# A pooled-attention and MLP kernel with its prologue rearranged: PSUM banks by hand, v in two parts, and small loads on other queues

## The chip, the cores and the metric

The kernel runs on one core of a Trainium2 chip. The metric is the device time of one execution in microseconds. The profile of one execution shows five engines: TensorE (PE, matmuls; PEld is its weight load), VectorE (DVE), ScalarE (ACT), GpSimd (POOL) and SyncE (SP), and sixteen DMA engines that they share. SP, ACT and POOL issue DMAs, each on a queue of its own: in the profile q1 is SyncE's, q10 ScalarE's and q0 GpSimd's.

## The reference

Eight batches of attention with eight heads; keys and values are averaged over groups of eight positions first. The result, one row of 512 numbers for each of 8 x 576 tokens, goes through an MLP with `h - tanh(h)` in the middle.

```python
batch, n_heads, seq, head_dim = (8, 8, 576, 64)      # pool = 8, so 72 pooled keys
k_p = k.reshape(B, H, Sp, pool, D).mean(axis=3)
v_p = v.reshape(B, H, Sp, pool, D).mean(axis=3)
scores = scale * np.matmul(q, k_p.transpose(0, 1, 3, 2))
attn = softmax(scores)                                # cut
attn_out = np.matmul(attn, v_p)
x = attn_out.transpose(0, 2, 1, 3).reshape(B * S, H * D)   # 4608 x 512
h = x @ w_in                                          # 512 x 2048
out = (h - np.tanh(h)) @ w_out                        # 2048 x 512
```

## The kernel before

Tokens are taken in nine groups of 512 for the MLP. For groups 1 to 8 the attention of the next batch is worked in between the MLP's matmuls. Group 0 has nothing before it, so the kernel opens with a prologue: load k, q and v of batch 0, pool and transpose them, compute scores, attention and x, and begin the MLP, while w_in (`w1b`), w_out (`w2b`) and batch 1 are on their way. `warm_pe` issues matmuls on zeros as filler for TensorE.

The loads of the prologue, in the order of the program (each engine runs its own in this order):

```python
# SyncE: keys of batch 0; ScalarE: queries of batch 0 but for the last 64 rows
load_main(k_pairs, k_raw[0], 0, 0, 1);  load_q0(0, 2)
load_main(k_pairs, k_raw[0], 0, 1, 2);  load_q0(2, 4)
load_main(k_pairs, k_raw[0], 0, 2, 4);  load_q0(4, 8)
load_dense(k_pairs, k_raw[0], 0, nc.scalar)
load_dense(v_pairs, v_raw[1], 0, nc.scalar)
...
nc.gpsimd.dma_start(out=v_bf[:, 0:NM, :], in_=v_pairs[0, 0:128, :, :])
...
for c in range(4):
    load_w1(c)                       # GpSimd: a quarter of w_in each, cast to bf16
load_w2(0)
nc.gpsimd.tensor_copy(out=v_bf[:, NM, :], in_=v_raw[1][:, NM, :])
load_w2(1)
nc.gpsimd.memset(k_raw[1][:, NM, :], 0.0)
nc.gpsimd.memset(v_raw[0][:, NM, :], 0.0)
nc.gpsimd.memset(KB[1][:, :], 0.0)

q_raws[1] = raw.tile(...)
after(load_k(1), w1_dmas[1])         # SyncE: keys of batch 1, once w1's second quarter is in
load_q(1, False)                     # SyncE
load_main(v_pairs, v_raw[1], 1, 0, NM)
```

The compute of the prologue:

```python
q_turn(...); k_turn(...); q_pe_transpose(...)         # cut
scores_wide(0, (0, 1))
nc.scalar.dma_start(out=t0[:QT, :, R, :], in_=q[0, :, QA:S, :].rearrange("h p d -> p h d"))
...                                                   # scores of the other keys, v pooled
load_left(v_pairs, v_raw[1], 1, nc.scalar)            # four small loads of batch 1
load_q_tail(1, q_raws[1], nc.scalar)

warm_pe(2, b0=3)
av_pair(0, 0, 2)                  # attention times v for two blocks of 128 tokens, one half
av_pair(1, 0, 5)                  # of the heads; VectorE then divides by the sum
av_pair(0, 1, 0)
warm_pe(1)
x0_turn((0, 1), 0, 7, nc.scalar.copy)   # transpose x by PE, copy it into xT
av_pair(1, 1, 2)
warm_pe(1)
x0_turn((2, 3), 0, 5, nc.scalar.copy)
warm_pe(2)
h_open(3, 4)                      # two of the four matmuls of an MLP tile, on 512 tokens
x0_turn((0, 1), 1, 7, nc.scalar.copy)
h_open(0, 0)
h_open(1, 1)
x0_turn((2,), 1, 5, nc.scalar.copy)
x0_turn((3,), 1, 6, nc.vector.tensor_copy)
h_open(2, 2)
h_open(4, 3)
nc.scalar.copy(out=q_bf[:QT, R, :, :], in_=t0[:QT, :, R, :])   # L740: cast of q's tail
for i in range(5):
    mlp_h_mms(0, i, 2, 4)         # the other two matmuls of the tile (L453)
    mlp_h_act(i, gts)             # ScalarE: tanh (L464); VectorE: gT = h - tanh(h) (L466)
for i in range(5, NHID):
    mlp_h(0, i, gts)              # all four matmuls; three PSUM banks in turn (ps_h)
    if i == 7:  q_pe_tail(0)      # reads q_bf's tail
    ...
pool_k(1, nc.gpsimd, mid=(2, 3))  # GpSimd: keys of batch 1, with load_w2(2), (3) in between
after(load_k(2), w2_dmas[2])
...
for u in range(16):               # second MLP product (L481), with batch 1's attention between
    ...
```

Of the kernel before, what the change touches and what calls it, by code (L numbers as in the profile page):

```python
# [8 lines left out]
FP32 = mybir.dt.float32  # L9
# [5 lines left out]
B, H, S, D = 8, 8, 576, 64  # L15
# [22 lines left out]
def kernel(  # L38
# [22 lines left out]
    def bank(i, shape):  # L61
        n = 1
        for d in shape[1:]:
            n *= d
        v = PS[:, i, 0:n]
        if len(shape) == 3:
            return v.rearrange("p (a b) -> p a b", a=shape[1])
        if len(shape) == 4:
            return v.rearrange("p (a b c) -> p a b c", a=shape[1], b=shape[2])
        return v  # L70
# [6 lines left out]
            self.n += 1  # L77
            return bank(self.ids[(self.n - 1) % len(self.ids)], shape)

    ps_h = Banks(0, 1, 2)  # L80
    ps_o = Banks(3, 4)
    ps_a = Banks(5, 6, 7)

    ctx.enter_context(tc.manual_schedule())

# [19 lines left out]
    VB = [const.tile([128, 3 * NM, D1], BF16, name=f"VB{i}") for i in range(2)]  # L105

    q_raws = {}
    rot = [0]

    def ps_any(shape, dtype, name):  # L110
        pool, tag = [(ps_a, "ps_a"), (ps_h, "hT_ps")][rot[0] % 2]
        rot[0] += 1
        return pool.tile(shape, dtype, name=name, tag=tag)

    evac_n = [0]

# [7 lines left out]
    def load_main(src, dst, b, t0, t1):  # L124
        return nc.sync.dma_start(out=dst[:, t0:t1, :], in_=src[b, 0:128, t0:t1, :])

    def load_left(src, dst, b, eng=nc.sync):
        return [
            eng.dma_start(out=dst[32 * t : 32 * t + LO, NM, :], in_=src[b, 128:PR, t, :])
            for t in range(NM)  # L130
        ]
# [17 lines left out]
    def load_q_tail(b, t, eng):  # L149
        eng.dma_start(  # L150
            out=t[:QT, :, R, :], in_=q[b, :, QA:S, :].rearrange("h p d -> p h d")
        )

    def load_q(b, tail=True):
        if b not in q_raws:
            q_raws[b] = raw.tile([128, H, R + 1, D], FP32, name="q_raw", tag="q_raw")
        t = q_raws[b]
        nc.sync.dma_start(
            out=t[:, :, 0:R, :], in_=q[b, :, 0:QA, :].rearrange("h (p j) d -> p h j d", j=R)
        )  # L160
        if tail:
            load_q_tail(b, t, nc.sync)

    qTs = {}
    kdups = {}
# [82 lines left out]
        v_main(VB[b % 2], r[:, :, 0:1, :], eng, 0, NM)  # L248
        v_left(VB[b % 2], r[:, NM, 0:1, :], eng)

    def v_main(vb, vs, eng, t0, t1):
        n = t1 - t0
        eng.tensor_tensor(
            out=vb[:, 2 * t0 : 2 * t1, 0:D].rearrange("p (t s) d -> p t s d", s=2),
            in0=vs[:, t0:t1, :, :].to_broadcast([128, n, 2, D]),
            in1=mask[:, 2 * t0 : 2 * t1, :]
            .rearrange("p (t s) o -> p t s o", s=2)
            .to_broadcast([128, n, 2, D]),
            op=ALU.mult,
        )  # L260

    def v_left(vb, vs, eng):
        eng.tensor_tensor(
            out=vb[:, 2 * NM :, 0:D],
            in0=vs.to_broadcast([128, NM, D]),
            in1=mask[:, 2 * NM :, :].to_broadcast([128, NM, D]),
            op=ALU.mult,
        )
# [179 lines left out]
    def mlp_h_mms(g, i, f0, f1, pool=None):  # L448
        tok0 = g * TG
        if f0 == 0:  # L450
            h_tiles[i] = ps_h.tile([128, TG]) if pool is None else pool
        for fb in range(f0, f1):
            nc.tensor.matmul(  # L453
                h_tiles[i][:, :],
                lhsT=w1b[:, fb, i * 128 : (i + 1) * 128],
                rhs=xT[:, fb, tok0 : tok0 + TG],
                start=(fb == 0),
                stop=(fb == NFB - 1),
            )

    def mlp_h_act(i, gts):
# [71 lines left out]
    def load_w2(c):  # L533
        w2_dmas.append(
            nc.gpsimd.dma_start(  # L535
                out=w2b[:, c * 4 : (c + 1) * 4, :], in_=w2_src[:, c * 4 : (c + 1) * 4, :]
            )
        )

    def after(lds, dep):  # L540
        for ld in lds:
            tc.add_manual_dep(
                ld.ins,
                dep.ins.name,
                mybir.DependencyInfo(mybir.DependencyClass.Sync, mybir.DependencyReason.DATA),
            )

    def warm_pe(n, cols=512, b0=4):
        for _ in range(n):
            nc.tensor.matmul(  # L550
                bank(b0, [128, cols]), lhsT=zeros[:, 0:128], rhs=zeros[:, 0:cols], start=True, stop=True
            )
# [52 lines left out]
    for c in range(4):  # L605
        load_w1(c)
    load_w2(0)
    nc.gpsimd.tensor_copy(out=v_bf[:, NM, :], in_=v_raw[1][:, NM, :])
    load_w2(1)
    nc.gpsimd.memset(k_raw[1][:, NM, :], 0.0)  # L610
    nc.gpsimd.memset(v_raw[0][:, NM, :], 0.0)
    nc.gpsimd.memset(KB[1][:, :], 0.0)

    q_raws[1] = raw.tile([128, H, R + 1, D], FP32, name="q_raw", tag="q_raw")
    after(load_k(1), w1_dmas[1])
    load_q(1, False)
    load_main(v_pairs, v_raw[1], 1, 0, NM)

    def k_turn(ta, tb):
# [5 lines left out]
    def k_turn_left():  # L625
        ps = ps_any([128, 128], FP32, "kT_ps")
        turn_tile(ps[:, :], kdups[0], NM)
        kb_left(KB[0], ps, nc.vector.tensor_copy)
# [3 lines left out]
    def q_turn(eng, h0, h1):  # L632
        eng(
            out=q_bf[:, 0:R, h0:h1, :].rearrange("p j h d -> p h j d"),
            in_=t0[:, h0:h1, 0:R, :],
        )

    def v_pe_pool(t0, t1, turn, b0=None):
        shape = [128, t1 - t0, 1, D]
        ps = ps_any(shape, FP32, "v_ps") if b0 is None else bank(b0, shape)  # L640
        for j in range(POOL):
            nc.tensor.matmul(
                ps[:, :, 0, :],
                lhsT=turn[:, :],
                rhs=v_bf[:, t0:t1, j * D : (j + 1) * D],
                start=(j == 0),
                stop=(j == POOL - 1),
            )
        return ps

    def ps_b1(shape, dtype, name):
        return ps_a.tile(shape, dtype, name=name, tag="ps_a")

    q_turn(nc.scalar.copy, 0, 2)
    q_turn(nc.scalar.copy, 2, 4)
    k_turn(0, 1)
    q_pe_transpose(0, (0,), "act")
    warm_pe(1)
    k_turn(1, 2)
    q_pe_transpose(0, (1,), "act")  # L660
    warm_pe(2)
    scores_wide(0, (0, 1))
    nc.scalar.dma_start(out=t0[:QT, :, R, :], in_=q[0, :, QA:S, :].rearrange("h p d -> p h d"))
    q_turn(nc.scalar.copy, 4, 6)
    q_turn(nc.scalar.copy, 6, 8)
    pool_k(0, nc.vector, 2, 4)
    warm_pe(6)
    k_turn(2, 4)
    pool_k(0, nc.vector, NM, NT)
    warm_pe(2)  # L670
    q_pe_transpose(0, (2, 3), "act")
    warm_pe(2)
    scores_wide(0, (2, 3))
    k_turn_left()
    warm_pe(2)
    v_ps = v_pe_pool(NM, NT, spread)
    scores_wide(0, (NM,))
    v_left(VB[0], v_ps[:, 0, :, :], nc.vector)
    vs = v_pe_pool(0, NM, ident, 4)
    v_main(VB[0], vs, nc.vector, 0, 2)  # L680
    v_main(VB[0], vs, nc.vector, 2, 4)
    load_left(v_pairs, v_raw[1], 1, nc.scalar)
    load_q_tail(1, q_raws[1], nc.scalar)
    gts = []

    def av_pair(p, half, b0):
        ps = PS[:, b0 : b0 + 2, 0 : 4 * D1].rearrange("p k (h d) -> p k h d", d=D1)
        for k in range(2):
            av_mms(0, 2 * p + k, half, ps[:, k, :, :])
        rden = work.tile([128, 2, 4, 1], FP32, name="rden2", tag="rden2")  # L690
        nc.vector.reciprocal(out=rden[:, :, :, :], in_=ps[:, :, :, D:D1])
        nc.vector.tensor_tensor(
            out=x0[:, 2 * p : 2 * p + 2, half, :, :],
            in0=ps[:, :, :, 0:D],
            in1=rden[:, :, :, :].to_broadcast([128, 2, 4, D]),
            op=ALU.mult,
        )
# [16 lines left out]
            in_=ps.rearrange("p f i c -> p f (i c)"),  # L714
        )

    def h_open(i, b0):
        mlp_h_mms(0, i, 0, 2, bank(b0, [128, TG]))

    warm_pe(2, b0=3)  # L720
    av_pair(0, 0, 2)
    av_pair(1, 0, 5)
    av_pair(0, 1, 0)
    warm_pe(1)
    x0_turn((0, 1), 0, 7, nc.scalar.copy)
    av_pair(1, 1, 2)
    warm_pe(1)
    x0_turn((2, 3), 0, 5, nc.scalar.copy)
    warm_pe(2)
    h_open(3, 4)  # L730
    x0_turn((0, 1), 1, 7, nc.scalar.copy)
    h_open(0, 0)
    h_open(1, 1)
    x0_turn((2,), 1, 5, nc.scalar.copy)
    x0_turn((3,), 1, 6, nc.vector.tensor_copy)
    h_open(2, 2)
    h_open(4, 3)
    ps_any = ps_b1
    ps_h.n = ps_o.n = 0
    nc.scalar.copy(out=q_bf[:QT, R, :, :], in_=t0[:QT, :, R, :])  # L740
# [113 lines left out]
```

The softmax here doesn't subtract the row's maximum and nothing guards it: scores larger than these inputs give would overflow.

## Time and profile before

| | |
|---|---|
| time, median of three runs | 300.99 us (300.81 to 301.04) |
| span of the profiled execution | 299.0 us |
| PE busy | 291.5 us (97%) |
| DVE, ACT, POOL busy | 158.4, 148.8, 115.7 us |
| HBM read, written | 36.70 MB, 9.44 MB |

A row of the timeline has the start in microseconds from the span's beginning, the length, the engine (with a q behind it: its sequencer, issuing a DMA), the line, the operation, what it writes and reads, the count, and in brackets how long the engine had been idle and what ended that. A row of the waits has who waited for whom, the total in microseconds, how often, and the longest. The landing of a DMA is counted from its issue.

### The profile page before, as it was taken

The page shows a single profiled execution, that of the slowest core. Times are in us where ns is not written, and L with a number is a line of the kernel's source. Part 1 is how long each engine was busy: PE and PEld are TensorE (multiplying, and loading weights), DVE is VectorE, ACT ScalarE, POOL GpSimd, SP SyncE. Part 2 cuts the span into 40 slices and gives each one's busy share as a digit, 9 for nine tenths or more (in the row PEclk, how much of TensorE's full clock was granted, in tenths as well). Part 3 has the DMA queues.
Part 4 walks back from the last instruction along what each step waited for, and adds up shares of the span by engine and source line. Part 5 has one row for each costly group of instructions (what it writes and reads, how often), then busy time and mean ns, then how long its engine had stood idle before and what let it go on. Part 6 is the DMA issues. An engine that isn't in the chain of part 4 may idle for free.

```text
span 299.0 us, 4704 instructions
## 1 busy us (share of the span) xinstructions
PE 291.5 (97%) x1672; PEld 142.8 (48%) x1672; DVE 158.4 (53%) x336; ACT 148.8 (50%) x279; POOL 115.7 (39%) x110
## 2 busy tenths in 40 slices
PE   7999999999999999999999999999999999999994
PEld 3454355544544454445544554455445544444443
DVE  5658665673547444753476247715680758008600
ACT  4647583666146623664266416651666066126511
POOL 8600906770396109913971099208930000000000
PEclk9999999999999999999999999999999999999999
DMA  7999999749955995699648974895431630111033
GB/s 259 221 211 280 310 235 328 233 89 331 233 109 109 290 283 129 109 297 250 105 89 236 313 166 88 265 294 137 89 66 35 90 96 0 37 70 36 2 70 70
DMA packets 66183, 49.79 MB, mean 167 GB/s; under 512 B 39920, under 2 KB 52976, under 8 KB 66160
## 3 DMA queue, kind: packets, MB, share of 16 engines
q1 hardware_dynamic: 58832, 42.94, 55.5%
q0 software_dynamic: 4752, 4.72, 9.5%
q10 hardware_dynamic: 2576, 1.84, 2.2%
q8 instruction: 13, 0.21, 0.3%
q14 instruction: 10, 0.08, 0.1%
HBM read 36.70 MB, written 9.44 MB: 154 GB/s over the span
## 4 chain that ended last, share of the span: by engine, by line
PE 85%; DMA 9%; POOL 4%; issue 0%; SPq 0%; ACT 0%; DVE 0%; POOLq 0%; DVEq 0%
PE PS L481 40%; PE PS L453 37%; DMA w1b<-in_moe_w_in_dram 4%; PE PS L368 4%; DMA k_raw<-in_k_dram 4%; PE PS L321 3%; POOL k_raw L221 1%; DMA out_dram<-o_sb 1%; POOL k_raw L226 1%; POOL kd L229 1%; POOL w2b L535 0%; PE PS L416 0%; POOL v_raw L599 0%; PE PS L194 0%; POOL w1b L528 0%
## 5 line engine op out<-in xcount | busy, mean ns | idle before, releaser
L481 PE MATMUL PS<-w2b,gT 128*128 128x512 bf16 x560 | 134.3, 379 | 0.0
L466 DVE TENSOR_TENSOR gT<-PS,t_sb 128x512 bf16<-128x512 f32 x144 | 98.9, 691 | 56.9 <-ACT t_sb L464 56.7
L453 PE MATMUL PS<-xT,w1b 128*128 128x512 bf16 x576 | 126.8, 379 | 0.6 <-ACT xT L712 0.6
L464 ACT ACTIVATE t_sb<-PS 128x512 f32<-128x512 f32 x144 | 85.6, 597 | 38.5 <-PE PS L453 37.7
L453 PEld LDWEIGHTS <-w1b 128*128 128x128 bf16 x576 | 55.9, 98 | 67.3 <-issue 0.8
L481 PEld LDWEIGHTS <-gT 128*128 128x128 bf16 x560 | 52.5, 98 | 52.0 <-issue 1.4
L490 ACT COPY o_sb<-PS 128x512 f32<-128x512 f32 x33 | 19.3, 586 | 75.2 <-PE PS L481 75.2
L385 DVE RECIPROCAL rden<-PS 128x4 f32<-128x4 f32 x72 | 12.8, 177 | 52.6 <-PE PS L368 52.3
L171 POOL CAST q_bf<-q_raw 128x2048 bf16<-128x2048 f32 x6 | 11.3, 1890 | 60.2 <-issue 34.2
L386 DVE TENSOR_TENSOR x_sb<-PS,rden 128x256 bf16<-128x256 f32 x72 | 30.6, 424 | 2.9 <-DMA xT<-x_sb 0.4
L221 POOL TENSOR_TENSOR k_raw<-k_raw 128x1280 f32<-128x1280 f32 x7 | 20.2, 2887 | 26.5 <-DMA k_raw<-in_k_dram 26.5
L340 ACT ACTIVATE E<-PS 128x288 bf16<-128x288 f32 x60 | 21.4, 409 | 13.2 <-PE PS L321 13.0
L368 PEld LDWEIGHTS <-E 128*128 128x128 bf16 x240 | 16.8, 98 | 8.3 <-issue 0.4
L368 PE MATMUL PS<-VB,E 128*128 128x130 bf16 x240 | 20.2, 220 | 0.1
L239 POOL TENSOR_TENSOR v_raw<-v_raw 128x1280 f32<-128x1280 f32 x6 | 17.4, 2900 | 0.0
L321 PE MATMUL PS<-qT,KB 128*128 128x288 bf16 (+5 forms) x128 | 17.0, 289 | 0.2
L321 PEld LDWEIGHTS <-KB 128*128 128x128 bf16 (+1 forms) x128 | 7.0, 96 | 10.2 <-issue 3.5
L550 PE MATMUL PS<-xT 128*128 128x512 bf16 x30 | 10.4, 463 | 1.3 <-DVE xT L562 1.3
L229 POOL TENSOR_TENSOR kd<-k_raw 128x640 bf16<-128x640 f32 x7 | 10.8, 1539 | 0.5
L226 POOL TENSOR_TENSOR k_raw<-k_raw 128x640 f32<-128x640 f32 x7 | 10.8, 1542 | 0.5
L242 POOL TENSOR_TENSOR v_raw<-v_raw 128x640 f32<-128x640 f32 x6 | 9.2, 1538 | 0.5
L272 POOL COPY KB<-kT 64x288 bf16<-64x288 bf16 x6 | 2.5, 418 | 13.8 <-DMA kT<-kd 13.8
(78 smaller groups left out, 107.1 us busy)
## 6 DMA issues: line engine op xcount, KB each, us to landing
k_raw<-in_k_dram SPq DMA_DIRECT2D x7, 1024.0 KB, 5.9
q_raw<-in_q_dram SPq DMA_DIRECT2D x7, 1024.0 KB, 10.2
v_raw<-in_v_dram SPq DMA_DIRECT2D x7, 1024.0 KB, 9.2
out_dram<-o_sb SPq DMA_DIRECT2D x38, 128.0 KB, 2.4
out_dram<-o_sb SPq DMA_DIRECT2D x16, 256.0 KB, 2.8
w1b<-in_moe_w_in_dram POOLq DMA_DIRECT2D x4, 512.0 KB, 13.7
w2b<-in_moe_w_out_dram POOLq DMA_DIRECT2D x4, 512.0 KB, 16.8
k_raw<-in_k_dram SPq DMA_DIRECT2D x7, 128.0 KB, 5.9
```

The lines of the kernel that those rows point to most:

```text
L221: first = eng.tensor_tensor(out=r[:, :, 0:4, :], in0=r[:, :, 0:4, :], in1=r[:, :, 4:8, :], op=ALU.add)
L226: eng.tensor_tensor(out=r[:, :, 0:2, :], in0=r[:, :, 0:2, :], in1=r[:, :, 2:4, :], op=ALU.add)
L239: eng.tensor_tensor(out=r[:, :, 0:4, :], in0=r[:, :, 0:4, :], in1=r[:, :, 4:8, :], op=ALU.add)
L321: nc.tensor.matmul(dst[p : p + w], lhsT=KB[b % 2][:, o : o + w], rhs=qTs[b][:, m, c0:c1], start=True, stop=True,)
L340: nc.scalar.activation(out=E[:, t, half * hs : (half + 1) * hs], in_=ps[:, :], func=ACT.Exp, scale=SCALE)
L368: nc.tensor.matmul(ps[:, 2 * n : 2 * n + 2, :].rearrange("p h d -> p (h d)") if n < 2 else ps.rearrange("p (a s) d -> p a s d", s=2)[:, :, ...
L386: nc.vector.tensor_tensor(out=x_sb[:, half, :, :], in0=ps[:, :, 0:D], in1=rden[:, :, :].to_broadcast([128, 4, D]), op=ALU.mult,)
L453: nc.tensor.matmul(h_tiles[i][:, :], lhsT=w1b[:, fb, i * 128 : (i + 1) * 128], rhs=xT[:, fb, tok0 : tok0 + TG], start=(fb == 0), stop=(fb ...
L464: nc.scalar.activation(out=t_sb[:, :], in_=h_ps[:, :], func=ACT.Tanh)
L466: nc.vector.tensor_sub(out=gT[:, :], in0=h_ps[:, :], in1=t_sb[:, :])
L481: nc.tensor.matmul(o_ps[:, :], lhsT=gts[i][:, tb * 128 : (tb + 1) * 128], rhs=w2b[:, i, :], start=(i == 0), stop=(i == NHID - 1),)
L490: (nc.vector.tensor_copy if g == 0 and tb % 2 else nc.scalar.copy)(out=o_sb[:, :], in_=o_ps[:, :])
```

## The change

The change touches the prologue only. PSUM banks of the prologue are named one by one (`plan`) rather than taken in turn from two pools, and the three groups of banks of the later MLP get other members. The v of batch 0 is pooled in two parts with banks of their own. MLP tiles 0, 1 and 2 are opened on the first 256 tokens as soon as these are transposed, and on the other 256 later. The two small loads of batch 1 (rest of v, tail of q) are issued by GpSimd rather than ScalarE, and the tail of q of batch 0 by SyncE rather than ScalarE. The keys of batch 1 wait for the first quarter of w1 rather than the second. The aim is an earlier start of the dense MLP and earlier keys for batch 1.

```diff
-    ps_h = Banks(0, 1, 2)
-    ps_o = Banks(3, 4)
-    ps_a = Banks(5, 6, 7)
+    ps_h = Banks(1, 3, 0)
+    ps_o = Banks(2, 5)
+    ps_a = Banks(4, 6, 7)
 ...
     load_w2(0)
+    nc.gpsimd.memset(k_raw[1][:, NM, :], 0.0)
+    nc.gpsimd.memset(KB[1][:, :], 0.0)
     nc.gpsimd.tensor_copy(out=v_bf[:, NM, :], in_=v_raw[1][:, NM, :])
     load_w2(1)
-    nc.gpsimd.memset(k_raw[1][:, NM, :], 0.0)
+    q_raws[1] = raw.tile([128, H, R + 1, D], FP32, name="q_raw", tag="q_raw")
+    load_left(v_pairs, v_raw[1], 1, nc.gpsimd)
+    load_q_tail(1, q_raws[1], nc.gpsimd)
     nc.gpsimd.memset(v_raw[0][:, NM, :], 0.0)
-    nc.gpsimd.memset(KB[1][:, :], 0.0)
-
-    q_raws[1] = raw.tile([128, H, R + 1, D], FP32, name="q_raw", tag="q_raw")
-    after(load_k(1), w1_dmas[1])
-    load_q(1, False)
+
+    after([load_main(k_pairs, k_raw[1], 1, 0, NM)], w1_dmas[0])
+    load_q_tail(0, t0, nc.sync)
+    load_dense(k_pairs, k_raw[1], 1)
+    after([load_q(1, False)], w1_dmas[2])
     load_main(v_pairs, v_raw[1], 1, 0, NM)
 ...
     scores_wide(0, (0, 1))
-    nc.scalar.dma_start(out=t0[:QT, :, R, :], in_=q[0, :, QA:S, :].rearrange("h p d -> p h d"))
 ...
-    vs = v_pe_pool(0, NM, ident, 4)
-    v_main(VB[0], vs, nc.vector, 0, 2)
-    v_main(VB[0], vs, nc.vector, 2, 4)
-    load_left(v_pairs, v_raw[1], 1, nc.scalar)
-    load_q_tail(1, q_raws[1], nc.scalar)
+    va = v_pe_pool(0, 2, ident, 5)
+    scores_wide(0, (NM,))
+    v_main(VB[0], va, nc.vector, 0, 2)
+    vc = v_pe_pool(2, NM, ident, 7)
+    v_main(VB[0], vc, nc.vector, 2, NM, 2)
 ...
-    warm_pe(2, b0=3)
-    av_pair(0, 0, 2)
-    av_pair(1, 0, 5)
-    av_pair(0, 1, 0)
-    warm_pe(1)
-    x0_turn((0, 1), 0, 7, nc.scalar.copy)
-    av_pair(1, 1, 2)
-    warm_pe(1)
-    x0_turn((2, 3), 0, 5, nc.scalar.copy)
-    warm_pe(2)
-    h_open(3, 4)
-    x0_turn((0, 1), 1, 7, nc.scalar.copy)
-    h_open(0, 0)
-    h_open(1, 1)
-    x0_turn((2,), 1, 5, nc.scalar.copy)
-    x0_turn((3,), 1, 6, nc.vector.tensor_copy)
-    h_open(2, 2)
-    h_open(4, 3)
+    av_pair(0, 0, 0)
+    av_pair(1, 0, 2)
+    av_pair(0, 1, 4)
+    av_pair(1, 1, 6)
+    x0_turn((0, 1), 0, 0, nc.scalar.copy)
+    warm_pe(2, b0=1)
+    h_open(0, 1, 0, 256)
+    x0_turn((2, 3), 0, 2, nc.scalar.copy)
+    h_open(1, 3, 0, 256)
+    h_open(2, 0, 0, 256)
+    x0_turn((0, 1), 1, 4, nc.scalar.copy)
+    h_open(0, 1, 256, 512)
+    h_open(1, 3, 256, 512)
+    h_open(2, 0, 256, 512)
+    h_open(3, 2, 0, 512)
+    x0_turn((2,), 1, 6, nc.scalar.copy)
+    x0_turn((3,), 1, 7, nc.vector.tensor_copy)
+    h_open(4, 5, 0, 512)
```

The cast of q's tail by ScalarE stays where it is, ahead of the first tanh.

More of the change, by code (lines that the diff above doesn't have):

```diff
@@ L107 @@
     q_raws = {}
-    rot = [0]
+    plan = []
     def ps_any(shape, dtype, name):
-        pool, tag = [(ps_a, "ps_a"), (ps_h, "hT_ps")][rot[0] % 2]
-        rot[0] += 1
-        return pool.tile(shape, dtype, name=name, tag=tag)
+        return bank(plan.pop(0), shape)
     evac_n = [0]
@@ L157, in load_q @@
         t = q_raws[b]
-        nc.sync.dma_start(
+        ld = nc.sync.dma_start(
             out=t[:, :, 0:R, :], in_=q[b, :, 0:QA, :].rearrange("h (p j) d -> p h j d", j=R)
@@ L162, in load_q @@
             load_q_tail(b, t, nc.sync)
+        return ld
     qTs = {}
@@ L249, in pool_v, with v_main @@
         v_left(VB[b % 2], r[:, NM, 0:1, :], eng)
-    def v_main(vb, vs, eng, t0, t1):
+    def v_main(vb, vs, eng, t0, t1, base=0):
         n = t1 - t0
@@ L254, in v_main @@
             out=vb[:, 2 * t0 : 2 * t1, 0:D].rearrange("p (t s) d -> p t s d", s=2),
-            in0=vs[:, t0:t1, :, :].to_broadcast([128, n, 2, D]),
+            in0=vs[:, t0 - base : t1 - base, :, :].to_broadcast([128, n, 2, D]),
             in1=mask[:, 2 * t0 : 2 * t1, :]
@@ L458, in mlp_h_mms @@
                 stop=(fb == NFB - 1),
+                skip_group_check=pool is not None or f0 > 0,
             )
@@ L652, in ps_b1 @@
         return ps_a.tile(shape, dtype, name=name, tag="ps_a")
+    plan += [0, 1, 2, 3, 4, 5, 6, 7, 0, 2, 4, 1, 3, 6]
     q_turn(nc.scalar.copy, 0, 2)
@@ L657 @@
     q_pe_transpose(0, (0,), "act")
-    warm_pe(1)
+    warm_pe(1, b0=7)
     k_turn(1, 2)
     q_pe_transpose(0, (1,), "act")
-    warm_pe(2)
+    warm_pe(2, b0=7)
     scores_wide(0, (0, 1))
-    nc.scalar.dma_start(out=t0[:QT, :, R, :], in_=q[0, :, QA:S, :].rearrange("h p d -> p h d"))
     q_turn(nc.scalar.copy, 4, 6)
@@ L666 @@
     pool_k(0, nc.vector, 2, 4)
-    warm_pe(6)
+    warm_pe(6, b0=7)
     k_turn(2, 4)
     pool_k(0, nc.vector, NM, NT)
-    warm_pe(2)
+    warm_pe(2, b0=3)
     q_pe_transpose(0, (2, 3), "act")
-    warm_pe(2)
+    warm_pe(2, b0=3)
     scores_wide(0, (2, 3))
+    v_ps = v_pe_pool(NM, NT, spread)
+    v_left(VB[0], v_ps[:, 0, :, :], nc.vector)
+    warm_pe(1, b0=6)
     k_turn_left()
-    warm_pe(2)
-    v_ps = v_pe_pool(NM, NT, spread)
+    va = v_pe_pool(0, 2, ident, 5)
     scores_wide(0, (NM,))
-    v_left(VB[0], v_ps[:, 0, :, :], nc.vector)
-    vs = v_pe_pool(0, NM, ident, 4)
-    v_main(VB[0], vs, nc.vector, 0, 2)
-    v_main(VB[0], vs, nc.vector, 2, 4)
-    load_left(v_pairs, v_raw[1], 1, nc.scalar)
-    load_q_tail(1, q_raws[1], nc.scalar)
+    v_main(VB[0], va, nc.vector, 0, 2)
+    vc = v_pe_pool(2, NM, ident, 7)
+    v_main(VB[0], vc, nc.vector, 2, NM, 2)
     gts = []
@@ L715, in x0_turn, with h_open @@
         )
-    def h_open(i, b0):
-        mlp_h_mms(0, i, 0, 2, bank(b0, [128, TG]))
-    warm_pe(2, b0=3)
-    av_pair(0, 0, 2)
-    av_pair(1, 0, 5)
-    av_pair(0, 1, 0)
-    warm_pe(1)
-    x0_turn((0, 1), 0, 7, nc.scalar.copy)
-    av_pair(1, 1, 2)
-    warm_pe(1)
-    x0_turn((2, 3), 0, 5, nc.scalar.copy)
-    warm_pe(2)
-    h_open(3, 4)
-    x0_turn((0, 1), 1, 7, nc.scalar.copy)
-    h_open(0, 0)
-    h_open(1, 1)
-    x0_turn((2,), 1, 5, nc.scalar.copy)
-    x0_turn((3,), 1, 6, nc.vector.tensor_copy)
-    h_open(2, 2)
-    h_open(4, 3)
+    def h_open(i, b0, c0, c1):
+        if c0 == 0:
+            h_tiles[i] = bank(b0, [128, TG])
+        for fb in range(2):
+            nc.tensor.matmul(
+                h_tiles[i][:, c0:c1],
+                lhsT=w1b[:, fb, i * 128 : (i + 1) * 128],
+                rhs=xT[:, fb, c0:c1],
+                start=(fb == 0 and c0 == 0),
+                stop=False,
+                skip_group_check=True,
+            )
+    av_pair(0, 0, 0)
[16 more added lines that the diff above has]
+    h_open(4, 5, 0, 512)
     ps_any = ps_b1
```

## The prediction

> **What bounds the kernel now.** I read the page first, then the waits, then the timeline of the first 40 us, because every changed line runs there. TensorE (PE) is busy 97% of the span. The waits of PE in the first 60 us are short:
>
> ```profile
> PE PS L282 <- POOL kd L229: 0.7, 1, 0.7
> PE PS L453 <- ACT xT L712: 0.6, 1, 0.6
> ```
>
> The first is the transposition of batch 1's keys waiting for GpSimd's pooling, the second the first MLP matmul waiting for x. After 55 us PE waits for nothing, so any shift of the start of the dense MLP goes to the end one to one. The start reads, from the timeline:
>
> ```profile
> 1.26 4.02 PE L550 MATMUL PS<-xT 128*128 128x512 bf16 x9 [1.26 <-DVE xT L562]
> 7.96 1.46 PE L550 MATMUL PS<-xT 128*128 128x512 bf16 x6
> 8.16 0.65 ACTq L663 DMA_DIRECT2D q_raw<-in_q_dram  x1
> ...
> 17.23 1.07 ACT L712 CAST xT<-PS 128x512 bf16<-128x512 f32 x2 [3.48 <-PE PS L368]
> 18.35 0.59 PE L453 MATMUL PS<-xT,w1b 128*128 128x512 bf16 x2 [0.55 <-ACT xT L712]
> ...
> 20.09 2.11 PE L453 MATMUL PS<-xT,w1b 128*128 128x512 bf16 x9
> 20.29 0.43 DVE L712 CAST xT<-PS 128x256 bf16<-128x256 f32 x1 [1.70 <-PE PS L704]
> 20.45 0.62 ACT L740 CAST q_bf<-q_raw 64x512 bf16<-64x512 f32 x1
> ...
> 21.59 0.60 ACT L464 ACTIVATE t_sb<-PS 128x512 f32<-128x512 f32 x1 [0.52 <-PE PS L453]
> ```
>
> The reader is to see two things. First, ScalarE casts q's last 64 rows (L740) right before the first tanh (L464). That load left at 8.16 on ScalarE's queue and landed 8.4 later (the answer for its line), at 16.6: in time. Second, nine filler matmuls took 4.02 us at the start, 447 ns each, and six took 1.46 at 7.96, 243 each: a cold PE runs at about half pace.
>
> The DMA engines are full from 5 to 55 us (share 1.1 to 1.2 in the five-microsecond windows). SyncE's queue:
>
> ```profile
> 18.45 0.38 SPq L125 DMA_DIRECT2D k_raw<-in_k_dram  x1
> 18.93 1.04 SPq L134 DMA_DIRECT2D k_raw<-in_k_dram  x1
> 20.02 0.57 SPq L158 DMA_DIRECT2D q_raw<-in_q_dram  x1
> ```
>
> By the answers for these lines the three land 10.3, 11.0 and 16.3 us after their issue: at 28.7, 29.9 and 36.3, one behind the other. The trace's DMA packets, counted by queue and size, say how: batch 1's keys (2048-byte packets) run from 22.29, 3.85 us after the issue, to 29.2, and only then q's 1024-byte packets from 28.7 to 35.8. While keys and weights both have work each gets 80 to 95 packets a microsecond; alone, the weights' queue gets 170 to 200.
>
> **What the Trainium skill says.** "DMA: Bandwidth & Descriptors", Queues, rings and completion order: SyncE and ScalarE each own one ring on each DMA engine, descriptors of a ring are consumed in order, and the engine takes turns between rings. The packet order above agrees. The same page, Issuing engines are not separate DMA queues: moving an issue to another engine saves only that sequencer's time; here that is 0.65 us per issue (L663). "TensorE: Matmul & The Clock Gate", its specifications table: ScalarE's queue is strict FIFO, so a cast that waits blocks every tanh behind it; no wait of this kind shows before. The same page, Part 1: after one idle window of about 3.4 us the PE clock halves, and about 3.4 us of work bring it back. The 447 and 243 ns agree with a slow start; a relapse is not seen before, since PE is never idle that long.
>
> **The change part by part.**
>
> (1) Banks by hand, v in two parts, MLP tiles opened on 256 tokens. Fillers drop from 30 to 25. The four attention-times-v groups now run back to back from about 14.6, as before. DVE still needs four times 0.20 + 0.69 = 3.6 us for the quotients from 15.1, so the last is ready at 18.6 either way (before: 17.90 + 0.69). Behind it the old order put an open tile ahead of the last transposes (19.87); the new one has opened its tiles by then. I put the last copy of x at 19.3 instead of 20.7. Gain on PE: 1.4 us, unless something else ends the wait.
>
> (2) The two small loads of batch 1 leave ScalarE's queue. This frees the issue at 16.56 that lay ahead of the x copy at 17.23: 0.6 us, contained in (1).
>
> (3) Batch 1's keys wait for the first quarter of w1 instead of the second. The first is issued at 5.13 and lands 10.1 later, 15.2; the second at 5.87 and 12.6 later, 18.4. The keys' issue moves 3.3 us forward. The wait of 0.7 us for pooled keys goes. But the weights behind then share the engines earlier.
>
> (4) The step I hold to be decisive: q's tail of batch 0, formerly issued at 8.16 on ScalarE's queue, is now issued by SyncE *behind* the keys' main load, which itself waits for w1. Its user is still the ScalarE cast ahead of the first tanh. Step by step:
> - w1's first quarter lands at about 15.0 (15.2 before; the tail's 512 packets no longer compete from 12.1 on, estimated 0.2).
> - keys issued at 15.1; first packet 3.85 later, as before: 18.9.
> - 512 key packets in turns with w1 at 92 per microsecond: 5.6, so 24.5.
> - the tail's 512 packets of 256 bytes behind them: before, beside w1, they ran from 12.12 to 16.1, 4.0 at most, and I take 3.7: 28.2.
> - from the last packet to landing, 0.5 as before (16.1 to 16.6): 28.7.
>
> Then cast 0.62, tanh 0.60, subtraction 0.69 (first and later DVE L466 rows), handovers about 0.1: the first gT is ready at 30.7. Five tiles are open and finish both halves without ScalarE. The sixth needs the bank of tile 0, so PE stands from about 21.7 to 30.7. Before, the sixth tile started after 20 matmuls of the MLP: 15 of them are in the rows up to 22.2, and five more at 0.216 from 21.82 make 22.9. Shift: 30.7 - 22.9 = 7.8.
>
> (5) Nine idle microseconds cool PE. About 4 us of work at half pace cost 2.0; some of it lies beside DVE's backlog of subtractions, so I take 1.7.
>
> Sum: + 7.8 (which swallows the 1.4 of part 1) + 1.7 - 0.7 (keys) = + 8.8. 301.0 + 8.8 = 309.8; I say 309.5, since other small waits of 34 to 38 us vanish as well. The later loads (w2, q and v of batch 1) arrive a few microseconds later than before by the same arithmetic, but PE reaches them 8 us later, so they should not bind.
>
> **Rivals.**
> A. *As meant*: the tail lands before 20 and part 1 shows. For it: the kernel's first loads landed 3.1 to 3.5 us after their issue, when the engines were free, and 15.7 + 3.5 = 19.2. Against it: the engines are full at 15, and the packet order shows the ring in order. It would give 301.0 - 1.4 - 0.7, about 299. 10%.
> B. *Tail not behind the keys, but late*: if the keys' packets don't hold it up, it still needs 3.85 of latency and 4 us of packets, 15.7 + 7.9 + 0.5 = 24; gT is ready at 26, the shift is 3.1, with less cooling 304 to 305. 10%.
> C. *Weights become the bound*: keys take half of the engines from 18.9, the third and fourth quarters of w1 come up to 1 to 2 us later, and GpSimd's later w2 issues wait for w2's first quarter in their turn. If ScalarE's wait were absent this would cost PE 1 to 2 us at tile 8 or 12 and give 300 to 302. With the wait it is hidden. It speaks for a result nearer zero only inside A.
>
> **Range and chances.** The centre rests on four terms, of which latency (3.85), sharing (5.6) and tail (3.7) are each good to about 0.7, and cooling to 0.8: 1.5 together, with the rivals pulling down. Range 305.0 to 311.5. Two per cent is 6.0 us, so slower begins at 307.0: my centre lies 2.5 above. Slower 0.76, same 0.23, faster 0.01.
>
> **What would show it.** In the changed profile: ScalarE's wait at the cast of q_bf, ended by the load of q_raw, 8 to 10 us long; PE's wait at its MLP matmul just before 30.7; a PE clock below full in a slice near 30 us; no PE wait for pooled keys. The last copy of x near 19.3 shows (1) right. The prediction is wrong if the cast starts before 24, or if the later matmuls wait for w1b or w2b instead.

## The result: 2.97% slower

The changed kernel takes 309.85 us (median of four executions, 309.68 to 310.33), the kernel before, run beside it, 300.9 (300.7 to 301.04). The ratio is 1.0297, 95% interval 1.0275 to 1.032. The profiled span is 308.2 us against 299.0.

The waits of PE up to 75 us, in the changed kernel (who waits, for whom, total, times, longest):

```profile
PE PS L452 <- DVE gT L466: 7.8, 1, 7.8
PE PS L367 <- DVE VB L262: 1.3, 1, 1.3
```

The wait of 0.7 us for the pooled keys of batch 1 is gone, and that of 0.6 for x is down to 0.2. In their place stand one of 7.8 for the subtraction behind the tanh, and one of 1.3 for v of batch 1. To see what stands behind the first, here is the timeline of the changed kernel from SyncE's issues to the second MLP product:

```profile
15.09 0.38 SPq L123 DMA_DIRECT2D k_raw<-in_k_dram  x1
15.52 0.75 SPq L148 DMA_DIRECT2D q_raw<-in_q_dram  x1
16.37 0.58 SPq L132 DMA_DIRECT2D k_raw<-in_k_dram  x1
...
28.36 0.62 ACT L753 CAST q_bf<-q_raw 64x512 bf16<-64x512 f32 x1 [8.51 <-DMA q_raw<-in_q_dram]
28.89 2.59 ACT L464 ACTIVATE t_sb<-PS 128x512 f32<-128x512 f32 x5
...
30.25 4.49 PE L452 MATMUL PS<-xT,w1b 128*128 128x512 bf16 x11 [7.84 <-DVE gT L466]
```

Read from the bottom: PE stops for 7.84 us for the first gT; ScalarE's first tanh starts at 28.89, because the cast ahead of it (L753, the old L740) stood 8.51 us waiting for q's tail; and that tail is the L148 issue at 15.52, the middle one of the three on SyncE. The view of that line gives its landing:

```profile
DMA to landing us min/median/max: 12.8/12.8/12.8
```

So 15.52 + 12.8 = 28.3, and the cast starts at once. The packets of SyncE's queue (q1), by size, show what the 12.8 us are made of:

```
q1, 2048 B (keys, 512 packets)     first 18.68   last 24.43
q1,  256 B (q's tail, 512 packets) first 24.14   last 27.84
```

Of the 12.8 us, 3.2 (from 15.52 to 18.68) pass before the queue's packets begin, 5.5 go to the keys ahead, 3.7 to the tail's own packets, and about half a microsecond lies between the last packet and the landing.

The path that sets the end thus runs through a load of 128 KB.

The clock. By stretches of the changed kernel (stretch, length, busy time of PE, PEld, DVE, ACT and POOL with instruction counts, granted PE clock, DMA share, GB/s):

```profile
27.00:30.25 3.25, 0.00 (x1) 0.00 (x0) 0.74 (x2) 1.89 (x4) 1.05 (x1) 0.50 1.18 247
30.25:34.00 3.75, 3.75 (x10) 1.39 (x10) 3.02 (x5) 1.97 (x5) 3.75 (x4) 0.53 1.16 276
```

PE does nothing from 22.41 (its row at 20.08 takes 2.33 us) up to 30.25 and meanwhile loses half its clock. The following 3.75 us hold ten matmuls, 375 ns each, at 0.53; before, a row of 26 such matmuls took 5.78 us, 222 ns each:

```profile
20.09 5.78 PE L453 MATMUL PS<-xT,w1b 128*128 128x512 bf16 x26
```

**Where the time went.** The first matmul of the second MLP product (L481), first before and then after:

```profile
34.24 2.75 PE L481 MATMUL PS<-w2b,gT 128*128 128x512 bf16 x12
...
43.03 2.75 PE L481 MATMUL PS<-w2b,gT 128*128 128x512 bf16 x12
```

It starts 8.79 us later. Behind it the old wait of 0.7 for keys goes and a new one of 1.3 comes: 8.79 - 0.69 + 1.33 = 9.43, against 9.2 in the spans and 8.95 in the times.

### The profile page after: what moved, and what is told of

The parts are those of the page before. It is cut to its first block, busy times and chain, and to the rows that moved or that the text cites. A ratio compares the mean times of both kernels' runs of the same rounds, so it can differ in the third digit from the quotient of the medians.

```text
span 308.2 us, 4703 instructions
## 1 busy us (share of the span) xinstructions
PE 290.8 (94%) x1649; PEld 143.7 (47%) x1681; DVE 163.7 (53%) x336; ACT 148.7 (48%) x279; POOL 118.9 (39%) x115
## 4 chain that ended last, share of the span: by engine, by line
PE 83%; DMA 8%; DVE 4%; POOL 1%; issue 1%; ACT 1%; SPq 0%; DVEq 0%; POOLq 0%
PE PS L452 39%; PE PS L481 37%; DMA q_raw<-in_q_dram 4%; PE PS L367 4%; DMA w1b<-in_moe_w_in_dram 3%; PE PS L320 3%; DVE v_raw L244 1%; DMA out_dram<-o_sb 1%; DVE VB L252 1%; DVE VB L262 1%; DVE v_raw L238 0%; DVE gT L466 0%; PE PS L415 0%; ACT t_sb L464 0%; POOL v_raw L599 0%
## 5 line engine op out<-in xcount | busy, mean ns | idle before, releaser
L452 PE MATMUL PS<-xT,w1b 128*128 128x512 bf16 x554 | 125.5, 383 | 8.6 <-DVE gT L466 7.8
L481 PE MATMUL PS<-w2b,gT 128*128 128x512 bf16 x542 | 131.7, 379 | 1.1 <-issue 0.2
L481 PEld LDWEIGHTS <-gT 128*128 128x128 bf16 x560 | 52.5, 98 | 52.0 <-issue 1.4
L490 ACT COPY o_sb<-PS 128x512 f32<-128x512 f32 x33 | 19.3, 585 | 75.2 <-PE PS L481 75.2
L170 POOL CAST q_bf<-q_raw 128x2048 bf16<-128x2048 f32 x6 | 11.3, 1888 | 57.9 <-issue 23.9
L238 POOL TENSOR_TENSOR v_raw<-v_raw 128x1280 f32<-128x1280 f32 x6 | 17.4, 2901 | 0.0
L550 PE MATMUL PS<-xT 128*128 128x512 bf16 x23 | 8.2, 485 | 1.3 <-DVE xT L562 1.3
```

The source lines that it names most:

```text
L238: eng.tensor_tensor(out=r[:, :, 0:4, :], in0=r[:, :, 0:4, :], in1=r[:, :, 4:8, :], op=ALU.add)
L452: nc.tensor.matmul(h_tiles[i][:, :], lhsT=w1b[:, fb, i * 128 : (i + 1) * 128], rhs=xT[:, fb, tok0 : tok0 + TG], start=(fb == 0), stop=(fb ...
L481: nc.tensor.matmul(o_ps[:, :], lhsT=gts[i][:, tb * 128 : (tb + 1) * 128], rhs=w2b[:, i, :], start=(i == 0), stop=(i == NHID - 1),)
L490: (nc.vector.tensor_copy if g == 0 and tb % 2 else nc.scalar.copy)(out=o_sb[:, :], in_=o_ps[:, :])
```

## The experiments

The theory: q's tail, queued behind the keys on SyncE, holds up ScalarE, which runs in order, so the tanh and with it PE; the rest of the change is worth one or two microseconds the other way. The rivals: the weights, loaded beside earlier keys, are the bound; the tail would be late on any queue; or it is the new order of PE's work and its banks. Times are medians; each ratio is to the kernel before, run beside it, with its 95% interval (it is not always the quotient of the two medians). "After" is the changed kernel.

| run | edit, in words | us | ratio |
|---|---|---|---|
| e1 | after, q's tail back on ScalarE | 300.89 | 0.9994 (0.9985 to 1.0003) |
| e9 | after, tail on SyncE ahead of the keys | 301.03 | 1.0002 (0.9993 to 1.0011) |
| e3 | after, cast of the tail moved behind tanhs | 300.67 | 0.9996 (0.9986 to 1.0006) |
| e4 | after, fillers in PE's idle time | 306.84 | 1.0199 (1.0178 to 1.0219) |
| e6 | after, keys of batch 2 later | 308.85 | 1.0253 (1.0218 to 1.0287) |
| e2 | before, tail on SyncE behind the keys | 319.92 | 1.0618 (1.0578 to 1.0658) |
| e5 | before, all three small loads moved | 313.99 | 1.043 (1.0389 to 1.047) |
| e7 | e1, q of batch 1 not held back | 301.32 | 1.0001 (0.9987 to 1.0015) |
| e8 | e7, keys held back as before | 300.49 | 0.9986 (0.997 to 1.0002) |
| e10 | e3, all keys ahead of the tail | 303.44 | 1.0065 (1.0044 to 1.0085) |
| e11 | e7, q's tail of batch 1 on SyncE | 300.26 | 0.9975 (0.9962 to 0.9987) |

### e1: the tail's load back where it was

```diff
-    load_q_tail(0, t0, nc.sync)
 ...
     scores_wide(0, (0, 1))
+    nc.scalar.dma_start(out=t0[:QT, :, R, :], in_=q[0, :, QA:S, :]...)
```

> The changed kernel with one load moved back: q's tail of batch 0 issued by ScalarE where it was before. Ring theory (the tail waits behind the keys in SyncE's ring, and ScalarE's cast waits for it): the 8.5 us wait of the cast, PE's 7.8 us wait and the half clock vanish; dense MLP from about 20.1 as against 20.95 before, keys' wait of 0.7 half gone: 299.9, between 299 and 300.8. Rival weights (the keys' earlier load takes the DMA engines from w1 and w2 and that is the loss): unchanged keys, so 306 or more. Rival banks (new PSUM banks and fewer fillers make PE wait or cool): 307 or more.

Measured: 300.89 us. One load accounts for the whole loss; the banks, the order of PE's work, the earlier keys and the other small loads cost nothing together. But they bring nothing either, though 1 us was expected (300.89 lies just outside the range). In the timeline of e1 the second product does start earlier, at 33.49, which is 0.75 us before the 34.24 of the kernel before. The waits of e1, other engines included, show where that went:

```profile
DVE v_raw L238 <- DMA v_raw<-in_v_dram: 5.6, 1, 5.6
...
ACT q_bf L170 <- DMA q_raw<-in_q_dram: 2.6, 1, 2.6
```

q and v of batch 1 now come late (the same two waits were 1.3 and 1.2 before): DVE waits for v until 43.21, where it pooled v from 40.35 before. PE gets three small waits of 0.6, 0.4 and 0.2 us for attention's operands. The gain is given back later.

### e9: the same queue, the other order

```diff
+    after([load_q_tail(0, t0, nc.sync)], kd0)      # kd0: batch 0's last keys have landed
     after([load_main(k_pairs, k_raw[1], 1, 0, NM)], w1_dmas[0])
-    load_q_tail(0, t0, nc.sync)
     load_dense(k_pairs, k_raw[1], 1)
```

> The changed kernel with two neighbours in SyncE's queue exchanged: q's tail of batch 0 goes out ahead of batch 1's keys, as soon as the last keys of batch 0 have landed (9.6). Same queue, same engine, same bytes. Ring theory: first packet at about 13.5, 512 packets in 4.0, landing at 17.9, before ScalarE reaches the cast at 19.9: no wait there; 300.9, between 300.4 and 301.3, as with the load on ScalarE. If SyncE's queue were slower as such for this load: the cast waits beyond 24, 305 or more.

Measured: 301.03 us, 8.8 below the changed kernel. The timeline of e9:

```profile
9.71 0.75 SPq L148 DMA_DIRECT2D q_raw<-in_q_dram  x1
14.92 0.39 SPq L123 DMA_DIRECT2D k_raw<-in_k_dram  x1
...
19.58 0.62 ACT L753 CAST q_bf<-q_raw 64x512 bf16<-64x512 f32 x1
```

The tail goes out ahead of the keys, lands 8.0 us later (17.7), and the cast has no idle time in front of it. SyncE's queue as such is harmless; the place in it, and the wait ahead of that place, cost 8.8 us. The run changes both at once, as the tail is also issued 5.8 us earlier (9.71 for 15.52). An estimate parts them: ahead of the keys but issued at 15.1, the tail would begin at 18.7, where the keys' packets began, and with its 3.7 and 0.5 us land near 22.9, about 3 us after ScalarE comes to its cast in e9. So the 5.5 us behind the keys are the larger part, and the wait for w1 is the rest; no run takes them apart.

### e3: let the tail be late, move its user

```diff
-    nc.scalar.copy(out=q_bf[:QT, R, :, :], in_=t0[:QT, :, R, :])
 ...
-        if i == 7:
+        if i == 10:
+            nc.scalar.copy(out=q_bf[:QT, R, :, :], in_=t0[:QT, :, R, :])
+        if i == 11:
             q_pe_tail(0)
 ...   # scores and attention of the tail four tiles later too, the transposition of its x behind the loop
```

> The changed kernel with all its loads, and ScalarE's cast of q's tail moved from ahead of the first tanh to behind the eleventh; what reads the cast (transposing q's tail, its scores, block 4 of the attention) moves four tiles later with it. Ring theory with the in-order ScalarE queue: the tail still lands at about 28.3, but nothing stands behind it; time 299.5 to 301, no PE wait over 1 us. If the late landing itself is not the cause but the share that the keys take of the DMA engines: still 306 or more.

Measured: 300.67 us. The tail of e3 lands at 28.1 (issued at 15.07, 13.0 us on the way), as late as in the changed kernel. The cast starts at that time, and no idle time of ScalarE stands in front of it:

```profile
28.12 0.62 ACT L761 CAST q_bf<-q_raw 64x512 bf16<-64x512 f32 x1
```

The late landing alone costs nothing. What costs is that the tanhs stand behind its user on an engine that runs in order. With e1 and e9 this settles the main point from three sides: another queue, another place in the queue, another place of the user.

### e4: keep PE busy while it waits

```diff
     for i in range(5): ...
+    warm_pe(34, b0=4)                              # before tile 5
```

> The changed kernel with 34 filler matmuls (34 x 0.216 = 7.3 us) between the second halves of tiles 0 to 4 and tile 5, inside PE's wait. Cooling theory: the clock stays full, the half-paced 3.5 us after the wait go, 1.4 to 1.8 us less: 308.2. Rival: the cooling is hidden beside VectorE's subtractions, within 0.3 us of the changed kernel: 309.6 to 310.1.

Measured: 306.84 us, 3.0 less than after, where 1.6 was expected. The timeline of e4:

```profile
30.21 2.75 PE L452 MATMUL PS<-xT,w1b 128*128 128x512 bf16 x12 [0.47 <-DVE gT L466]
...
41.49 2.75 PE L481 MATMUL PS<-w2b,gT 128*128 128x512 bf16 x12
```

The sixth tile starts at the same time as in the changed kernel (30.21 and 30.25), but the second product at 41.49 instead of 43.03. So the cooling alone is worth about 1.5 us. The other half of the 3.0 is the 1.3 us wait for v, which is gone too: starting 1.5 us earlier, DVE was at the last step of its work on v (49.12 to 49.54) when GpSimd began on its keys at 49.32. That pointed to e6.

### e6: is the second wait a collision of DVE and GpSimd?

```diff
-    after(load_k(2), w2_dmas[2])
+    after(load_k(2), w2_dmas[3])
```

> The changed kernel, with batch 2's keys loaded after w2's last quarter rather than its third, so that GpSimd pools them from about 52 us and not while VectorE pools v of batch 1 (47 to 51). Collision theory (two engines slow each other down when both work on SBUF at once): VectorE's last three steps take 0.49, 0.69 and 0.42 us as before instead of 3.06, 1.91 and 1.75, PE's wait of 1.3 us near 55 goes: 308.5. Rival: VectorE's long steps come from something else (its data, a wait of its own) and stay: 309.5 to 310.

Measured: 308.85 us, 1.0 less than after, but the four executions lie between 307.88 and 310.11, and the two intervals of the ratio overlap (1.0218 to 1.0287, 1.0275 to 1.032). It is the trace that decides. The same instructions, first in the changed kernel:

```profile
49.33 2.91 POOL L220 TENSOR_TENSOR k_raw<-k_raw 128x1280 f32<-128x1280 f32 x1 [12.51 <-DMA k_raw<-in_k_dram]
49.53 3.06 DVE L244 TENSOR_TENSOR v_raw<-v_raw 128x320 f32<-128x320 f32 x1
52.32 1.67 POOL L225 TENSOR_TENSOR k_raw<-k_raw 128x640 f32<-128x640 f32 x1
52.63 1.91 DVE L252 TENSOR_TENSOR VB<-v_raw,mask 128x512 bf16<-128x512 f32 x1
54.07 1.86 POOL L228 TENSOR_TENSOR kd<-k_raw 128x640 bf16<-128x640 f32 x1
54.46 1.75 DVE L262 TENSOR_TENSOR VB<-v_raw,mask 128x256 bf16<-128x256 f32 x1
56.27 0.39 PE L367 MATMUL PS<-VB,E 128*128 128x130 bf16 x4 [1.33 <-DVE VB L262]
```

and then in e6:

```profile
49.44 0.49 DVE L244 TENSOR_TENSOR v_raw<-v_raw 128x320 f32<-128x320 f32 x1
49.97 0.69 DVE L252 TENSOR_TENSOR VB<-v_raw,mask 128x512 bf16<-128x512 f32 x1
50.58 0.42 DVE L262 TENSOR_TENSOR VB<-v_raw,mask 128x256 bf16<-128x256 f32 x1
51.38 2.89 POOL L220 TENSOR_TENSOR k_raw<-k_raw 128x1280 f32<-128x1280 f32 x1 [14.42 <-DMA k_raw<-in_k_dram]
```

Same shapes, same program, only GpSimd's work moved by two microseconds: DVE's three instructions take 1.6 us in all instead of 6.7. In the changed kernel each ends 0.3 to 0.6 us after the GpSimd instruction that had begun before it. The Trainium skill, "SBUF — State Buffer", Who interferes with whom, names it: a DVE instruction with two SBUF inputs takes its second one through a read port that it shares with GpSimd, and a GpSimd instruction that reads SBUF needs the same port; the one that comes second is blocked until the first has ended. The trace agrees, 0.49 us becoming 3.06 beside one of 2.91. Before the change DVE had finished at 44.3, and GpSimd began at 47.66: 3.4 us apart. The shift of PE by nine microseconds took DVE's v along by 6.8 (from 40.35 to 47.14), but the keys of batch 2, which wait for a load of w2, by only 1.7 (from 47.66 to 49.33). So the two met.

### e2: the tail moved in the kernel before

```diff
-    after(load_k(1), w1_dmas[1])
+    after([load_main(k_pairs, k_raw[1], 1, 0, NM)], w1_dmas[1])
+    load_q_tail(0, t0, nc.sync)
+    load_dense(k_pairs, k_raw[1], 1)
 ...
-    nc.scalar.dma_start(out=t0[:QT, :, R, :], in_=q[0, :, QA:S, :]...)
```

> The kernel before with one load moved: q's tail of batch 0 issued by SyncE behind batch 1's keys, which still wait for w1's second quarter. Nothing else of the change. Ring theory: keys issued at 18.45 as before, their packets 22.3 to 28.0, the tail's 3.7 us more and 0.5 to land, about 32.2; that is 3.9 us later than in the changed kernel, so the cast starts at 32.2, PE's sixth tile at 34.1 as against 22.9, plus 1.7 of cooling, less 0.7 for keys: 313, between 311 and 315. Rivals weights and banks: neither is touched, so 301 to 302.

Measured: 319.92 us, 7 above what was expected, and not by the expected path. The timeline of e2:

```profile
27.46 0.65 ACTq L150 DMA_DIRECT2D q_raw<-in_q_dram  x1
28.15 1.07 ACT L713 CAST xT<-PS 128x512 bf16<-128x512 f32 x2 [14.47 <-DMA k_raw<-in_k_dram]
```

ScalarE's issue of the *other* small load, q's tail of batch 1, waited until 27.46 for the keys of batch 1, with which it has nothing to do. The copy of x stood behind it: ScalarE had computed nothing for 14.47 us, and PE waited 11.5 us for x. The trace has the reason. The loads of SyncE and ScalarE signal eight semaphores between them (counters that a landing raises and that others wait for; numbers 100, 102 and 104 to 109), those of GpSimd another eight (111 to 118), and an issue can have to wait for the very semaphore that it is to signal. In the kernel before, batch 1's q tail waits for number 100, which belonged to batch 0's q tail on the same engine; in e2 number 100 has gone to the keys of batch 1. Moving one load gave later ones other semaphores. So e2 does not tell the theories apart, since x itself was late; it shows the same trap with an issue in place of a cast. DVE and GpSimd collided in it too, with a PE wait of 3.0 us for VB.

### e5: the tail moved in the kernel before, without that side effect

```diff
+    load_left(v_pairs, v_raw[1], 1, nc.gpsimd)     # behind load_w2(1), as in the change
+    load_q_tail(1, q_raws[1], nc.gpsimd)
 ...
-    load_left(v_pairs, v_raw[1], 1, nc.scalar)
-    load_q_tail(1, q_raws[1], nc.scalar)
 ...   # and the edits of e2
```

> The kernel before, with the tail of q of batch 0 on SyncE behind the keys as in the run before, and the two small loads of batch 1 on GpSimd as in the changed kernel, so that ScalarE issues nothing that can wait. Keys still after w1's second quarter. Ring theory: keys issued at about 17.6 (the second quarter lands sooner without the tail beside it), first packet 3.6 later, keys 5.75, tail 3.7, landing 0.5: the cast starts at 31.1, 2.7 us later than in the changed kernel, PE's sixth tile at 33.0. 301 + 10.1 + 1.4 of cooling - 0.7 for keys + 1.3 to 3.0 for the meeting of VectorE and GpSimd near 50 us: 314, between 312.5 and 315.5. If the tail does not wait in the ring: 301 to 302.

Measured: 313.99 us, as expected. The timeline of e5:

```profile
30.50 0.62 ACT L741 CAST q_bf<-q_raw 64x512 bf16<-64x512 f32 x1 [10.40 <-DMA q_raw<-in_q_dram]
```

Old banks, old order of PE, keys at their old time: the cast waits even longer, until 30.50 (31.1 expected), since the keys ahead of it go out later: at 17.22 for 15.09, 2.13 us, and the cast is 2.14 us later. PE waits 9.6 us for gT, and another 1.5 for VB. That rules out banks and PE's order as the cause, and shows the loss to follow the time of the keys' issue.

### e7 and e8: where does the gain of e1 go?

e7 frees q of batch 1 of its wait for w1's third quarter; e8 puts in addition the keys' wait back to the second quarter.

```diff
-    after([load_q(1, False)], w1_dmas[2])
+    load_q(1, False)                                                     # e7, on e1
 ...
-    after([load_main(k_pairs, k_raw[1], 1, 0, NM)], w1_dmas[0])
+    after([load_main(k_pairs, k_raw[1], 1, 0, NM)], w1_dmas[1])          # e8, on e7
```

> The changed kernel with q's tail back on ScalarE, and q of batch 1 no longer waiting for w1's third quarter. Theory: the run without this edit gained 0.75 us by 33.5 us and lost it at 38 to 47 to q of batch 1 (cast at 36.9 as against 36.3) and v (pooled from 43.2 as against 40.3); SyncE's ring stood empty for some 2 us before q. Without the gate both land about 2 us sooner: 300.2, between 299.8 and 300.5. Rival: the DMA engines are full either way, so what q gains w2 loses: 300.9.

> As the run before, and batch 1's keys after w1's second quarter as in the kernel before: all large loads in the old order, the rest of the change kept. Theory: the start of the dense MLP is 0.75 us sooner, but pooled keys come when they came before (37.6), so PE waits for them 0.75 longer: 300.9, between 300.6 and 301.1. Rival (keys are not what ends the wait there): 300.2.

Measured: 301.32 and 300.49 us. e7 missed: no gain. ScalarE's cast of q starts 1.2 us earlier than in e1 (35.69), but now it is q's tail of batch 1 that is late. From the timeline of e7:

```profile
40.37 0.62 ACT L174 CAST q_bf<-q_raw 64x512 bf16<-64x512 f32 x1 [2.69 <-DMA q_raw<-in_q_dram]
```

PE waits 1.8 us for the transposed q behind it. PE's other long wait in e7, 1.1 us for keys, ends at 10.43 and is for batch 0's keys, ahead of anything that the edit touches. The expectation of e11 below takes it for a wait for batch 1's pooled keys; for those PE does not wait in e7. This profile simply starts late: attention's first product with v begins at 14.82, in the other runs with the changed prologue between 13.67 and 14.14, and the second product only at 34.26. So differences of half a microsecond between single profiles say little here. It is the median that shows e7 to bring no gain.

In e8 PE waits 0.6 us for batch 1's keys and 0.4 for q, and v is pooled from 42.14, against 40.35 before. 300.49 lies just below the expected range, nearer to its rival; but the interval of e8 includes 1 and overlaps that of e7, so a gain of e8 over either is not shown.

What e7 won on q it lost on q's tail. The DMA engines are full up to here (share 1.12 to 1.24 from 15 to 40 us in e7), so a load that goes first delays another. The tail, on GpSimd's queue, is issued at 22.94 in e7, earlier than the 23.49 of e1, but lands 17.4 us later, against 14.7. The time of its issue hangs on shared semaphores as well. In the changed kernel's timeline:

```profile
15.36 0.48 POOL L127 DMA_DIRECT2D v_raw<-in_v_dram  x1 [2.04 <-DMA w1b<-in_moe_w_in_dram]
...
21.83 0.72 POOL L148 DMA_DIRECT2D q_raw<-in_q_dram  x1 [3.45 <-DMA w1b<-in_moe_w_in_dram]
```

These two issues of GpSimd, and another at 17.90, wait for landings of w1, with whose data they have nothing to do.

### e10: late cast and all keys first

```diff
+    load_dense(k_pairs, k_raw[1], 1)
     load_q_tail(0, t0, nc.sync)
-    load_dense(k_pairs, k_raw[1], 1)
 ...   # on e3; cast one tile later still (i == 11), x's last transposition at u == 1
```

> From the run with the late cast: the rest of the keys of batch 1 goes ahead of q's tail in the ring, the cast stands behind the twelfth tanh, its users one tile later, and block 4's x is transposed in the second product's second unit, where VectorE has it ready. Aim: a version that beats both kernels. Theory: PE's 1.1 us of waits for VectorE's x go, pooled keys are ready at 33.6, but q of batch 1 still lands near 37 and takes back a part: 300.2, between 299.8 and 300.5. If the DMA engines alone set the time at 37 to 43: 300.7, as with the late cast before.

Measured: 303.44 us, a miss of 3.2. The timeline of ScalarE in e10:

```profile
37.80 1.99 ACT L170 CAST q_bf<-q_raw 128x1024 bf16<-128x1024 f32 x2 [4.12 <-DMA q_raw<-in_q_dram]
```

By moving x's last transposition to u == 1 I had put its copy on ScalarE (L422) behind the cast of batch 1's q (L170), which stands 4.12 us waiting for its load. PE waited 2.8 us for that copy, and its granted clock was 0.60 from 40.6 to 44 us, so cooling adds to the loss. It is the trap of the change once more, at another place and by my own edit; whether the order of keys and tail brings anything is not told by this run.

### e11: what the runs pointed to

```diff
-    load_q_tail(1, q_raws[1], nc.gpsimd)
 ...
-    load_q(1, False)
+    load_q(1)                                      # with its tail, on SyncE behind the main part
 ...
-    pool_k(1, nc.gpsimd, mid=(2, 3))
+    pool_k(1, nc.gpsimd)
+    load_w2(2)
+    load_w2(3)                                     # on e7
```

> From the run with q of batch 1 ungated: q's tail of batch 1 moves from GpSimd to SyncE behind q's main load, and GpSimd pools batch 1's keys without the two issues of w2 in between, which follow. Aim: a version that beats both kernels. Theory: the waits there were 1.1 us for pooled keys, because GpSimd stood before its second w2 issue, and 1.8 us for q's tail, which landed at 40.3 behind w2 in GpSimd's ring; both go; pooled keys at 32 to 33, q's tail at about 38, v near 41, the second product from 33.5 as against 34.24: 299.7, between 299.2 and 300.2. Rival: the DMA engines are full until 41, so v or w2 lands later and takes the gain: 300.7 to 301.2.

Measured: 300.26 us, just above the expected range; ratio 0.9975 (0.9962 to 0.9987): faster than both kernels, against the one before by about 0.75 us, between 0.4 and 1.1. From its timeline:

```profile
34.56 1.99 ACT L170 CAST q_bf<-q_raw 128x1024 bf16<-128x1024 f32 x2 [0.17 <-DMA q_raw<-in_q_dram]
```

The keys are pooled at 32.3, q is ready in time, the second product starts at 33.59, and the waits of PE up to 75 us are at most 0.4 each, but for the one at the start that every run has. So the rearranged prologue gains together with these further edits, and none of its loads holds up PE for long. How much of the gain is the prologue's own is not shown: e11 also moves q, its tail and two loads of w2, and these edits were not tried on the kernel before. The edit of GpSimd's pooling was made against a wait that e7 did not have.

## Why the prediction was right, and where its sum was not

The predicted 309.5 (305.0 to 311.5) holds the measured 309.85, and by the mechanism named as decisive. By its own steps:

- **The tail's way, step (4).** Keys issued at 15.1, measured 15.09; first packet 18.9, measured 18.68; keys' packets to 24.5, measured 24.43; tail landed 28.7, measured 28.3; first gT at 30.7, and PE went on at 30.25. The 22.9 that the prediction gives for the sixth tile before is a slip: it is the start of the twentieth matmul, and the sixth tile begins with the next, the fifteenth of the 26 in the row from 20.09 above, at 20.09 + 14 x 0.216 = 23.1. By the prediction's own numbers the shift was 7.6, and it came out as 30.25 - 23.1 = 7.15. PE stood from 22.41, not 21.7, so it was idle for 7.84 us, not nine. e1, e3 and e9 show that without this wait the loss is nil. What carried this step was the packet order of the trace of before, not the issue times.
- **Cooling, step (5).** 1.7, measured about 1.5 by e4, and the drop to half clock, which no profile of before showed, is there (0.50 from 27 us on). 7.15 + 1.5 = 8.65, against 8.79 seen at the second product.
- **Keys, step (3).** The 0.7 us wait went, as predicted. But the price of it, put at nothing ("they should not bind"), is only hidden by the late start: in e1, q and v of batch 1 do bind.
- **Part (1), mis-sized.** The last copy of x was put at 19.3, 1.4 sooner than before. It ended at 20.02, 0.7 sooner than the 20.72 before. The failed premise is "the new one has opened its tiles by then". In the changed kernel's timeline eight opening matmuls stand ahead of the last transposes:

```profile
18.09 1.25 PE L724 MATMUL PS<-xT,w1b 128*128 128x256 bf16 x8
19.17 0.39 PE L707 MATMUL PS<-ident,x 128*128 128x128 bf16 x4
...
19.60 0.42 DVE L715 CAST xT<-PS 128x256 bf16<-128x256 f32 x1 [1.40 <-PE PS L707]
20.08 2.33 PE L452 MATMUL PS<-xT,w1b 128*128 128x512 bf16 x10
```

 The old order had an open tile in that place, the new one has another. The second halves start at 20.08 against 20.95, 0.9 sooner. Of this, 0.7 stands already at attention's first product with v (13.92 against 14.60), which the prediction had at the same time as before. So the sign that was named for this part, the last copy near 19.3, did not appear. In this result the error doesn't show, as the big wait swallows part (1).
- **A term left out.** The sum had no collision of DVE and GpSimd: + 1.3 in the profile, 1.0 by the medians of e6. And I had written that after 55 us PE waits for nothing; after the change it does, at 56.27. That the total still fits is partly luck: the shift (7.15 for 7.8) and the cooling (1.5 for 1.7) together took about 0.85 off, the collision put 1.0 to 1.3 on, and the net of 0.15 to 0.45 is about the 0.35 by which 309.5 was short. Whether the 0.3 that I took off for "other small waits" is real, the runs don't tell.
- **The rivals.** A fell with the landing at 28.3; B with the packets, which queue behind the keys. C (300 to 302 without ScalarE's wait) is about what e1 measures, but by another load than named: not the quarters of w1, but q and v of batch 1. How far each of the three reordered loads accounts for e1's lost 0.75 us, the runs leave open, since freeing one delayed another.

## What to carry to other kernels

A small load belongs ahead of the large ones on its queue, and its user behind everything on its engine that doesn't need it: either alone was worth the whole 8.8 us here (e9, where the load was also freed of its wait, and e3). When a shift of several microseconds is predicted, ask next which pairs of DVE and GpSimd work, apart until now, it brings together, and which loads it makes late for the following stage. Before moving a DMA issue to another engine, look at what that engine's later issues will then wait for.

## What the runs showed of the hardware that was not expected

- A DVE instruction of 0.49 us took 3.06 beside one of GpSimd, and two more went from 0.69 and 0.42 to 1.91 and 1.75; GpSimd's own grew little (2.89 to 2.91, 1.54 to 1.67 and 1.86).
- Between the issue of the keys on SyncE and their first packet 3.6 us passed in the changed kernel (15.09 to 18.68) while the DMA engines were full.
- Shorter waits cool PE too than the idle window of about 3.4 us that the prediction quotes: one of 2.84 us in e10 was followed by a granted clock of 0.60 (40.6 to 44 us), one of 3.04 in e2 by 0.50 (62.2 to 65.5). Waits of 1.33 in the changed kernel and 1.5 in e5 left it at 1.00.
- The issue of a load can hold up its engine for long: in e2, ScalarE computed nothing for 14.47 us, most of it behind an issue that waited for a load of unrelated data, and in the changed kernel GpSimd stood 2.0, 2.1 and 3.5 us before three such issues. This comes of how the compiled program shares its semaphores among the loads.
